# Seven of 24 key tiles exponentiated on VectorE, and reloads with earlier priorities, in a planned four-block transformer kernel

## The chip, the cores and the metric

One core of a Trainium2 chip runs the whole program in one launch. The metric is the device time of one execution in microseconds (us), taken as the median of three runs.

## The reference

Four residual blocks follow each other on x of 2048 rows by 1024 columns in bf16: linear attention (A), softmax attention (B), A and B again, with the same weights the second time. Each block first applies a layer norm. There are 32 heads of 32 columns.

```python
# block A
pq = einsum("bhsd,hdf->bhsf", q, w_phi); pk = einsum("bhsd,hdf->bhsf", k, w_phi)
phi_q = concat([softmax(pq), softmax(-pq)]); phi_k = concat([softmax(pk), softmax(-pk)])
kv = einsum("bhsf,bhsd->bhfd", phi_k, v);  z = sum over s of phi_k
o = (phi_q @ kv) / (phi_q . z + 1e-6);     x = x + o @ wo
# block B
scores = q @ k^T * 32**-0.5;  x = x + (softmax(scores) @ v) @ wo
```

For the change it matters that a key tile of block A needs two exponentials, exp(k) and exp(-k), and that block B needs the exponential of 32 x 2048 x 2048 scores each time.

## The kernel before

The program isn't written in the order in which it runs. Every operation (a group of matmuls, an activation, a DMA) is recorded with an engine, a duration that the planner assumes, the operations it depends on, its buffers and a priority; `Sched.run` then lays them out in time, and the instructions are issued in the order that this planner found. A buffer comes from one SBUF arena or from the eight PSUM banks, with a quota for each class. So a number in the table at the top of the file (a due time, a step, a limit) can shift the order of everything that follows. Each engine then runs its own list strictly in order, and waits where an operand isn't there.

Attention (block B) is cut into 32 turns, one for each pair of a 512-row query chunk and a group of four heads. A turn has 64 score tiles of 128 keys by 512 queries. TensorE makes three or four of them at once, each in 32 rows of the array (L1280). ScalarE takes the exponentials of two or three score tiles in one instruction (L1338, 128x1024 or 128x1536). One or two more tiles of a group go to VectorE, which converts them with a tensor_scalar (L1436) to 16-bit numbers whose bits are a power of two; when two such tiles have come together, `exp_dve` mends the mantissa with two masks (L1241) and two tensor_tensors (L1246). Score matrices are scaled by 2^7/ln 2 for that, and ScalarE's exponential is given the factor `e_scale` that undoes it. Then TensorE multiplies with the values and with ones (L1479). `MIX` says how many groups must lie between two groups in which ScalarE gets two tiles and VectorE the third; `MOST` limits VectorE's tiles in a turn.

TensorE's time between the scores is filled with other matmuls (L642, four at once in 32 columns each): key, value and query projections of later heads, output projections, and, in the first attention alone, the keys and values of the second linear layer. Those are made for three row chunks with eight key tiles each, 24 in all, by `a_keys` with `alone`: TensorE makes the tile, VectorE copies it out of PSUM (L874), ScalarE takes both exponentials (L878), VectorE sums them by head (L882), inverts the sums (L885) and scales the values by them (L891), and TensorE adds to the state (L913). The fourth chunk is made after the first attention, with the first layer's method. Where the planner sees TensorE with too little to do, it adds matmuls that nobody reads: four at once on `onesD` or `zero`, one at a time on `onesD` (L642, L1737, L1732, each reading `xR`).

A turn ends with VectorE's copy of the result out of PSUM (L1494) and, by a detour through DRAM (`rd`), a division: L1541 multiplies by the inverse that SyncE's queue brought back (L1528, L1534, L1536). The output projection is added to the residual in L1212. All DMAs are issued from SyncE's one queue. Ahead of the second linear layer's queries it reads back slabs of the folded query weights (`wd_q`, eight DMAs) and two chunks of normed rows (`xd`, eight DMAs, L1609).

## Time and profile before

| | before |
|---|---|
| median of three runs | 2135.45 us (2132.93 to 2135.77) |
| the profiled execution's own time | 2136.92 us |
| its span, first to last instruction | 2135.1 us |
| mean granted clock of TensorE | 0.996 |
| busy: TensorE, ScalarE, VectorE | 2086.7, 1904.7, 1772.2 us |

The stretches of the span: up to 310 us the first linear layer and what leads into attention; 310 to 1163 us the first attention; 1163 to 1390 us the rest of the second linear layer; 1390 to 2122 us the second attention; then the last output tiles. Busy times are of the hardware profiler; an activation's record reaches into that of the next one, so single durations add up to more than the busy time of the engine. The spacing of starts tells what one costs. A granted clock below 1 means that TensorE's matmuls were slowed.

### The profile page before, as it was taken

To read this page: it belongs to the slowest core of one execution; us is meant where nothing else is said; L and a number is where in the kernel's file an instruction comes from. 1 tells how busy PE (TensorE), PEld (TensorE's weight loads), DVE (VectorE), ACT (ScalarE), POOL (GpSimd) and SP (SyncE) were. 2 spreads that over 40 slices of the span, in tenths; PEclk is the share of its full clock that TensorE was granted. 3 is DMA by queue.
4 is the path that set the end of the run, shared out by engine and by line. 5 is a ranking of instruction groups with operands and counts; after the bars stand their busy time and mean duration, and the time that the engine had idled before them with its cause. 6 is when DMAs were issued, how large, how long until landed. Compare 5 with 4: busy or idle time off the path is not lost. (4 is left out here: it accounts for less than half of the span.)

```text
span 2135.1 us, 65137 instructions
## 1 busy us (share of the span) xinstructions
PE 2086.7 (98%) x27811; PEld 787.5 (37%) x27811; DVE 1772.2 (83%) x3305; ACT 1904.7 (89%) x2029; POOL 26.6 (1%) x83
## 2 busy tenths in 40 slices
PE   8999999999999999999999999999999999999999
PEld 5543443333333333333333434533333333333333
DVE  8866545757566899999998876698899999999998
ACT  7437769989999999999999577799999999999998
POOL 1000000000000000000000000000000000000000
PEclk9999999999999999999999999999999999999999
DMA  8720321131233322442455403211111122121111
GB/s 234 163 72 21 94 58 29 34 73 49 61 76 96 101 86 75 132 144 66 102 155 153 112 27 83 70 28 32 33 45 43 42 51 63 47 75 52 51 47 37
DMA packets 255467, 160.78 MB, mean 75 GB/s; under 512 B 147784, under 2 KB 229704, under 8 KB 255176
## 3 DMA queue, kind: packets, MB, share of 16 engines
q1 hardware_dynamic: 255176, 156.62, 27.5%
q8 instruction: 217, 3.56, 0.7%
q14 instruction: 74, 0.61, 0.1%
HBM read 89.72 MB, written 29.87 MB: 56 GB/s over the span
## 5 line engine op out<-in xcount | busy, mean ns | idle before, releaser
L1338 ACT ACTIVATE arena<-psum 128x1536 bf16<-128x1536 f32 (+1 forms) x1332 | 1559.3, 1437 | 28.0 <-PE psum L1280 20.0
L642 PE MATMUL psum<-arena 128*32 128x512 bf16 (+1 forms) x9536 | 634.6, 366 | 10.7 <-DVE arena L1212 2.6
L1479 PE MATMUL psum<-arena 128*32 128x512 bf16 x4096 | 606.3, 383 | 1.8 <-DVE arena L1494 1.4
L1479 PE MATMUL psum<-arena,ones_bf 128*32 128x512 bf16 x4096 | 606.4, 383 | 0.0
L1280 PE MATMUL psum<-arena 32*128 32x512 bf16 x4096 | 524.5, 384 | 24.9 <-ACT arena L1338 17.6
L1436 DVE TENSOR_SCALAR arena<-psum 128x512 uint16<-128x512 f32 x662 | 444.8, 681 | 80.9 <-PE psum L1280 76.6
L638 PE MATMUL psum<-arena 128*128 128x512 bf16 (+1 forms) x1968 | 430.5, 373 | 0.9 <-DMA arena<-in_A_wqkv_dram 0.4
L1280 PEld LDWEIGHTS <-arena 32*128 32x128 bf16 x4096 | 160.5, 91 | 551.8 <-issue 548.1
L642 PEld LDWEIGHTS <-arena 128*32 128x32 bf16 x9536 | 209.4, 95 | 262.2 <-issue 163.9
L638 PEld LDWEIGHTS <-arena 128*128 128x128 bf16 x1968 | 185.9, 98 | 220.4 <-issue 22.1
L1241 DVE TENSOR_SCALAR work<-arena 128x1024 uint16<-128x1024 uint16 (+1 forms) x668 | 261.8, 414 | 2.3
L1479 PEld LDWEIGHTS <-arena 128*32 128x32 bf16 x4096 | 167.7, 95 | 213.1 <-issue 146.9
L1246 DVE TENSOR_TENSOR arena<-work 128x1024 bf16<-128x1024 bf16 x334 | 225.7, 676 | 2.6
L1246 DVE TENSOR_TENSOR work<-arena,work 128x1024 bf16<-128x1024 bf16 x334 | 225.5, 675 | 0.0
L1479 PEld LDWEIGHTS <-ones_bf 128*32 128x32 bf16 x4096 | 166.1, 95 | 22.3 <-issue 4.0
L878 ACT ACTIVATE arena<-psum 128x512 bf16<-128x512 f32 x80 | 43.7, 595 | 75.1 <-PE psum L638 69.9
L1143 DVE CAST arena<-psum 128x512 bf16<-128x512 f32 (+1 forms) x120 | 69.2, 577 | 43.3 <-PE psum L642 43.2
L1494 DVE COPY arena<-psum 128x512 f32<-128x512 f32 x126 | 85.8, 681 | 11.5 <-PE psum L1479 11.4
L882 DVE TENSOR_REDUCE arena<-arena 128x32 f32<-128x1024 bf16 x64 | 77.4, 1209 | 16.0 <-ACT arena L878 14.3
L1038 ACT ACTIVATE arena<-psum 128x512 bf16<-128x512 f32 x112 | 60.7, 617 | 26.4 <-PE psum L638 22.5
L891 DVE TENSOR_TENSOR arena<-psum,arena 128x1024 bf16<-128x1024 f32 x64 | 78.1, 1220 | 2.6
L683 ACT ACTIVATE arena<-xR 128x1024 bf16<-128x1024 bf16 x40 | 42.4, 1065 | 36.4 <-DVE xR L1117 36.4
(103 smaller groups left out, 997.7 us busy)
## 6 DMA issues: line engine op xcount, KB each, us to landing
arena<-in_B_wqkv_dram SPq DMA_DIRECT2D x66, 256.0 KB
arena<-rd SPq DMA_DIRECT2D x62, 256.0 KB
xa<-arena SPq DMA_DIRECT2D x48, 256.0 KB
arena<-in_A_wqkv_dram SPq DMA_DIRECT2D x40, 256.0 KB
arena<-in_B_wo_dram SPq DMA_DIRECT2D x40, 256.0 KB
arena<-arena SPq DMA_DIRECT2D x256, 32.0 KB
arena<-wd_k SPq DMA_DIRECT2D x32, 256.0 KB
arena<-arena SPq DMA_DIRECT2D x62, 128.0 KB
```

The costliest lines, as they stand in the source:

```text
L638: nc.tensor.matmul(out_, lhsT=lhsT, rhs=rhs, start=start, stop=stop, skip_group_check=True)
L642: nc.tensor.matmul(out_[ks, :], lhsT=lhsT[:, ks], rhs=rhs, start=start, stop=stop, tile_position=(0, 32 * k), skip_group_check=True)
L882: red = op("DVE", dve_us(1024) + 0.107, lambda ev=ev, sv=sv: nc.vector.reduce_sum(out=sv(), in_=ev().rearrange("p s (h d) -> p (s h) d", d ...
L891: ml = op("DVE", dve_us(1024), lambda vpv=vpv, wv_=wv_, sv=sv: nc.vector.tensor_tensor(out=wv_()[:, :, :, 0:DH], in0=vpv().rearrange("p (h ...
L1143: return soon(op("DVE", dve_us(n), lambda: nc.vector.tensor_copy(out=dst(), in_=src()), [dep], bufs, prio))
L1241: return sch.later("DVE", n * C512 / 3840 + 0.065, lambda: nc.vector.tensor_scalar(out=out_().bitcast(U16), in0=y_v().bitcast(U16), scalar ...
L1246: return sch.later("DVE", n * C512 / 1920 + 0.065, lambda: nc.vector.tensor_tensor(out=out_(), in0=in0(), in1=in1(), op=what), deps, [e_b, ...
L1280: nc.tensor.matmul(out=out_, lhsT=kT[g][1]()[r, pp, d * P:(d + 1) * P], rhs=q_of[(qc, g)][1]()[r, (pp + j // 2) % 2, :], start=True, stop= ...
L1338: ex = make("ACT", act_us(w * C512), lambda: nc.scalar.activation(out=e_v()[:, 0:w * C512], in_=s_v()[:, 0:w * C512], func=ACT.Exp, scale= ...
L1436: pair["got"].append(sch.later("DVE", dve_us(512), lambda: nc.vector.tensor_scalar(out=e_v().bitcast(U16)[:, k, :], in0=s_v(), scalar1=EXP ...
L1479: nc.tensor.matmul(out=a_v()[col:col + 32, :], lhsT=v_v()[:, kc % 4, o:o + DH] if what == 0 else ones_bf[:], rhs=ev()[:, x * C512:(x + 1) ...
L1494: cp = op("DVE", dve_us(512), lambda t_v=t_v, a_v=a_v: nc.vector.tensor_copy(out=t_v(), in_=a_v()), [last], [a_b, t_b], prio - 4)
```

## The change

Seven key tiles (the last three of chunk 0, the last three of chunk 1, the last of chunk 2) don't go to ScalarE. VectorE converts the key tile straight out of PSUM, makes the negated one from it, and runs `exp_dve` on both at once. For this the folded key weights are scaled by 2^7/ln 2 in `fold_phi`, by the same 16 evictions as before, and the exponentials that stay on ScalarE use `e_scale` and its negative.

```diff
+KEY_DVE = (3, 3, 1, 0)
+XR = 40
+SL = 30
-MIX = (lambda i: (1, 2, 1, 0)[i // 8], lambda i: (0, 0, 1, 0)[i // 8])
+MIX = (lambda i: (1, 2, 1, 2)[i // 8], lambda i: (0, 0, 1, 0)[i // 8])
-MOST = (lambda i: 1 if i < 1 else 12, lambda i: 24 if i < 1 else 29)
+MOST = (lambda i: 3 if i < 1 else 12, lambda i: 24 if i < 1 else 27)
-END = 32
+END = 28
-         "e": 6, "vp": 6, "e1": 4, "vp1": 4, ...
+         "e": 6, "vp": 6, "e1": 5, "vp1": 4, ...
...
+                by_dve = alone and 4 * fc + t >= 8 - KEY_DVE[c]
+                if by_dve:
+                    k1 = op("DVE", dve_us(512), lambda kpv=kpv, ev=ev: nc.vector.tensor_scalar(
+                        out=ev().bitcast(U16)[:, 0, :], in0=kpv(), scalar1=EXP2_OFF * ONE, scalar2=0.0,
+                        op0=ALU.add, op1=ALU.max), [k1], [kp, eb], pr)
+                    soon(k1)
+                elif alone:
...
-                ex = [op("ACT", act_us(512), lambda s=s, kpv=kpv, ev=ev: nc.scalar.activation(
-                    out=ev()[:, s, :], in_=kpv(), func=ACT.Exp, scale=(1.0, -1.0)[s]),
+                ex = [] if by_dve else [op("ACT", act_us(512), lambda s=s, kpv=kpv, ev=ev: nc.scalar.activation(
+                    out=ev()[:, s, :], in_=kpv(), func=ACT.Exp, scale=(e_scale, -e_scale)[s]),
...
+                        n = sch.later("DVE", C512 / 3840 + 0.065, lambda: nc.vector.tensor_scalar(
+                            out=ev().bitcast(U16)[:, 1, :], in0=ev().bitcast(U16)[:, 0, :], scalar1=-1.0,
+                            scalar2=2 * EXP2_OFF * ONE, op0=ALU.mult, op1=ALU.add), [o], [eb], pr)
+                        exp_dve({"got": [o, n], "bufs": (eb,), "e": ev}, pr).out.append(red)
...
-            wq_s = [slab("slab", second - 15 + fc, ...
+            wq_s = [slab("slab", second - SL + fc, ...
-                xnA[c] = (x_b, x_v, [dma(second - 20 + 20 * c, ...
+                xnA[c] = (x_b, x_v, [dma(second - XR + 20 * c, ...
```

Some fifteen more numbers of the table change by a little: due times of the second attention's key, value and late query tiles (KS, VH, V_LATE, Q_LATE), of output projections (GAPS, OUT_AT, GO, WO), and limits (SLACK, OPEN, MOST_E, NEAR).

What the planner makes of it, counted in the two built programs:

| | before | after |
|---|---|---|
| ScalarE, three score tiles in one (L1338, 128x1536) | 770 | 812 |
| ScalarE, two score tiles in one (128x1024) | 562 | 518 |
| ScalarE, exponentials of keys (L878) | 128 | 114 |
| VectorE, score tiles converted (L1436) | 662 | 624 |
| VectorE, pairs mended (two L1241, two L1246 of 128x1024) | 328 | 315, seven of them keys |
| VectorE, single tiles mended | 6 | 8 |
| TensorE, passes of three or four scores | 1332 | 1330 |
| TensorE, unread passes: onesD in columns, zero, onesD whole | 111, 51, 47 | 90, 64, 45 |

All of the difference in ScalarE's and nearly all in VectorE's counts lies in the first attention; the second has 368 and 283 of ScalarE's two kinds in both programs. Of the first attention's 32 turns the last sixteen have 41 more of the three-tile kind, 42 fewer of the two-tile kind and 41 fewer score tiles on VectorE. All other matmuls are the same in number, in another order from the first turns on. On SyncE's queue the eight `wd_q` reads now stand ahead of the last-but-one turn's `rd` write (L1534), where all eight stood behind it; the eight `xd` reads stand where they stood, behind the last `qf` and `in_B_wqkv` reads.

VectorE, chunk 1's sixth key tile, in turn 24, lines of before: the key tile is copied (L874), and summed (L882) when ScalarE has made its exponentials; the products of an earlier tile (L891) lie between.

```order
L874 COPY arena<-psum 128x512
L1436 TENSOR_SCALAR arena<-psum 128x512
L1246 TENSOR_TENSOR work<-arena,work 128x1024
L1436 TENSOR_SCALAR arena<-psum 128x512
L882 TENSOR_REDUCE arena<-arena 128x32
L891 TENSOR_TENSOR arena<-psum,arena 128x32x32
L885 RECIPROCAL arena<-arena 128x32
```

The same tile of VectorE after the change, where L1260 and L1265 are the masks and products of `exp_dve`, L1455 a score tile, and L891, L910 and L904 the sum, the scaled values and the inverse:

```order
L878 TENSOR_SCALAR arena<-psum 128x512
L899 TENSOR_SCALAR arena<-arena 128x512
L1260 TENSOR_SCALAR work<-arena 128x1024 x2
L1265 TENSOR_TENSOR work<-arena,work 128x1024
L1265 TENSOR_TENSOR arena<-work 128x1024
L1455 TENSOR_SCALAR arena<-psum 128x512
L891 TENSOR_REDUCE arena<-arena 128x32
L910 TENSOR_TENSOR arena<-psum,arena 128x32x32
L904 RECIPROCAL arena<-arena 128x32
```

A conversion stands in the copy's place, and five instructions more stand between it and the sum.

ScalarE in the last quarter of the first attention, before, from 1090 us of the span on; the width tells whether two or three score tiles are taken:

```order
L1338 ACTIVATE arena<-psum 128x1536
L1338 ACTIVATE arena<-psum 128x1024 x4
L1338 ACTIVATE arena<-psum 128x1536 x2
L878 ACTIVATE arena<-arena 128x512 x2
L1338 ACTIVATE arena<-psum 128x1536 x2
L1338 ACTIVATE arena<-psum 128x1024 x2
L1338 ACTIVATE arena<-psum 128x1536
L1338 ACTIVATE arena<-psum 128x1024 x5
```

ScalarE at about the same place after the change (L1357 is L1338, L887 is L878):

```order
L1357 ACTIVATE arena<-psum 128x1536
L1357 ACTIVATE arena<-psum 128x1024
L1357 ACTIVATE arena<-psum 128x1536 x2
L1357 ACTIVATE arena<-psum 128x1024
L1357 ACTIVATE arena<-psum 128x1536 x2
L887 ACTIVATE arena<-arena 128x512 x2
L1357 ACTIVATE arena<-psum 128x1024
```

With MIX at 2 one two-tile instruction is followed by two of three tiles; before they could follow each other.

VectorE where the first attention ends, before: L1541 is the division of the turn before the last, which needs the `rd` read; L1212 evicts an output projection; L1494 is the last turn's copy, and L1504 its inverse.

```order
L1212 TENSOR_TENSOR arena<-xR,psum 128x512
L1246 TENSOR_TENSOR arena<-work 128x1024
L1541 TENSOR_TENSOR arena<-arena 128x512
L1212 TENSOR_TENSOR arena<-xR,psum 128x512
L1494 COPY arena<-psum 128x512
L1504 RECIPROCAL arena<-arena 64x128 x2
```

VectorE at the same place after the change (L1231 is L1212, L1513 is L1494, L1523 is L1504, L1560 is L1541):

```order
L944 TENSOR_TENSOR arena<-arena,psum 128x264
L1552 RECIPROCAL arena<-arena 128x16
L1231 TENSOR_TENSOR arena<-xR,psum 128x512 x2
L1513 COPY arena<-psum 128x512
L1523 RECIPROCAL arena<-arena 64x128 x2
L1231 TENSOR_TENSOR arena<-xR,psum 128x512
L1560 TENSOR_TENSOR arena<-arena 128x512
```

The division that needs the read now stands behind three evictions, the last copy and two inversions.

More of the change, by code (lines that the diff above doesn't have):

```diff
@@ L438 @@
 KL = (17.0, 31.56)
-KS = (2.41, 4.25)
+KS = (2.41, 5.55)
 VS = (4.26, 6.75)
@@ L447 @@
 LN_PE = (3, 3)
[L448 removed]
+WO = 8.18
 KD = 12.15
 HALF = (False, True)
[L451 to L453 removed]
+VH = 3.31
+V_LATE = (None, ((21.96, 6.48), (59.37, 7.17)))
+Q_LATE = (lambda c, g: 104.52 + 4.56 * g if c == 2 else -5.67 + 18.61 * g, lambda c, g: 151.84 + 11.78 * g)
 QL = (11, 9.91)
 AW = 26
[L456 to L457 removed]
+OUT_AT = (228.3, 247.14, 267.11)
+GO = 3.17
 BO = 296.78
@@ L752, in turned_slab, with fold_phi @@
         return b, v, [got[0] + got[1], got[2] + got[3]] * 2
-    def fold_phi(col, wd_v, prio, use_pe, after=()):
+    def fold_phi(col, wd_v, prio, use_pe, after=(), by=1.0):
         w_t = []
@@ L800, in fold_phi @@
                 if eng == "ACT":
-                    e = op("ACT", act_us(512), lambda m=m, pv=pv, s_v=s_v: nc.scalar.copy(
-                        out=s_v()[:, m, :], in_=pv()), [a], [pb, s_b], prio + 0.01)
-                else:
-                    e = soon(op("DVE", dve_us(512), lambda m=m, pv=pv, s_v=s_v: nc.vector.tensor_copy(
-                        out=s_v()[:, m, :], in_=pv()), [a], [pb, s_b], prio + 0.01))
+                    e = op("ACT", act_us(512), lambda m=m, pv=pv, s_v=s_v: nc.scalar.activation(
+                        out=s_v()[:, m, :], in_=pv(), func=ACT.Copy, scale=by), [a], [pb, s_b], prio + 0.01)
+                else:
+                    e = soon(op("DVE", dve_us(512), lambda m=m, pv=pv, s_v=s_v: nc.vector.tensor_scalar(
+                        out=s_v()[:, m, :], in0=pv(), scalar1=by, scalar2=None, op0=ALU.mult), [a], [pb, s_b], prio + 0.01))
                 parts.append(e)
@@ L1604 @@
         else:
-            wq_s = [slab("slab", second - 15 + fc, wdq_v[:, :, fc * C512:(fc + 1) * C512], C512, [store["q"][fc]])
+            wq_s = [slab("slab", second - SL + fc, wdq_v[:, :, fc * C512:(fc + 1) * C512], C512, [store["q"][fc]])
                     for fc in range(2)]
```

32 lines of the change are left out of this document (15 added, 17 removed).

## The prediction, as it was put on record

> **What bounds the kernel now.** I read the view of windows first, one window for each stage; the two middle columns that matter are busy us of VectorE (third) and ScalarE (fourth), the one before the last but one is TensorE's granted clock. The chain of waits is of no use here: it follows the last eleven microseconds alone.
>
> ```profile
> core 0: us, PE busy (x) PEld busy (x) DVE busy (x) ACT busy (x) POOL busy (x), PEclk, DMA share, GB/s
> 310.00:540.00 230.00, 227.17 (x3111) 78.92 (x3109) 144.34 (x262) 215.74 (x184) 0.00 (x0) 1.00 0.19 47
> 540.00:744.00 204.00, 199.44 (x2779) 65.45 (x2776) 136.76 (x254) 201.50 (x168) 0.00 (x0) 0.99 0.31 84
> 744.00:855.00 111.00, 105.67 (x1590) 36.95 (x1594) 103.12 (x184) 107.09 (x103) 3.16 (x8) 1.00 0.28 79
> 855.00:960.00 105.00, 101.64 (x1491) 33.50 (x1483) 97.74 (x181) 101.06 (x96) 1.83 (x4) 0.98 0.49 140
> 960.00:1066.00 106.00, 104.04 (x1682) 37.02 (x1680) 105.77 (x201) 102.48 (x98) 1.58 (x4) 1.00 0.32 83
> 1066.00:1163.00 97.00, 93.66 (x1539) 33.28 (x1539) 93.67 (x169) 94.89 (x93) 3.06 (x8) 1.00 0.50 135
> 1163.00:1390.00 227.00, 222.67 (x2055) 97.91 (x2058) 162.17 (x301) 156.31 (x291) 2.81 (x8) 0.98 0.31 84
> 1390.00:2122.00 732.00, 717.34 (x10555) 253.84 (x10547) 703.84 (x1366) 731.66 (x631) 0.00 (x0) 1.00 0.17 46
> ```
>
> Three regimes. In the second attention (1390 to 2122) ScalarE is busy for 731.66 of 732 us: it is the bound, and there is nothing else to win. From 540 to 744 VectorE has a third of its time free, and ScalarE, at 201.50 of 204, still sets the pace. From 744 to 1163, where key tiles of the second linear layer are made, all engines are near full: VectorE 103.12 + 97.74 + 105.77 + 93.67 = 400.3 of 419 us, in one window 105.77 of 106; ScalarE 107.09 + 101.06 + 102.48 + 94.89 = 405.5. ScalarE's idle 13.5 us there are what a better balance could win.
>
> What ended that idle time, in the view of waits for ScalarE from 744 to 1163 us (us in total, times, longest):
>
> ```profile
> ACT arena L1338 <- PE psum L1280: 9.0, 13, 2.1
> ACT arena L1338 <- PE psum L642: 1.7, 3, 1.1
> ACT arena L1338 <- PE psum L1479: 1.6, 2, 1.2
> ```
>
> ScalarE waits for scores, so for TensorE. TensorE's records overlap, so its share of busy time says little; the timeline of TensorE gives the price of a pass by starts:
>
> ```profile
> 1501.63 0.39 PE L1280 MATMUL psum<-arena 32*128 32x512 bf16 x3
> 1501.95 1.05 PE L642 MATMUL psum<-arena 128*32 128x512 bf16 x16
> 1502.93 0.39 PE L1280 MATMUL psum<-arena 32*128 32x512 bf16 x3
> ```
>
> Sixteen column matmuls are four passes. Scores to the next kind take 0.32 us, four passes and the change back 0.98: with two equal changes of kind that is about 0.22 a pass and 0.10 a change.
>
> **The change part by part.** First the balance of 744 to 1163. The timelines of ScalarE and VectorE price one instruction (start, time, count):
>
> ```profile
> 977.08 4.13 ACT L1338 ACTIVATE arena<-psum 128x1536 bf16<-128x1536 f32 x3
> 984.78 2.90 ACT L1338 ACTIVATE arena<-psum 128x1024 bf16<-128x1024 f32 x3
> 1089.81 1.34 ACT L878 ACTIVATE arena<-arena 128x512 bf16<-128x512 f32 x2
> 1090.85 8.00 ACT L1338 ACTIVATE arena<-psum 128x1536 bf16<-128x1536 f32 x7
> ...
> 982.51 0.41 DVE L1241 TENSOR_SCALAR work<-arena 128x1024 uint16<-128x1024 uint16 x1
> 982.85 0.68 DVE L874 COPY arena<-psum 128x512 f32<-128x512 f32 x1
> 983.45 0.67 DVE L1436 TENSOR_SCALAR arena<-psum 128x512 uint16<-128x512 f32 x1
> 984.05 0.67 DVE L1246 TENSOR_TENSOR work<-arena,work 128x1024 bf16<-128x1024 bf16 x1
> 984.65 0.68 DVE L1436 TENSOR_SCALAR arena<-psum 128x512 uint16<-128x512 f32 x1
> ...
> L1241 DVE TENSOR_SCALAR work<-arena 128x512 uint16<-128x512 uint16 x12 | 3.0, 282 | 0.0
> ```
>
> ScalarE: three tiles in one cost 4.13 / 3 = 1.38 us, two tiles 2.90 / 3 = 0.97, a key's exponential (1090.85 - 1089.81) / 2 = 0.52. In the whole program 42 more of the first, 44 fewer of the second, 14 fewer of the third: 58.0 - 42.7 - 7.3 = **8.0 us more** work, nearly all in the last sixteen turns, so in 744 to 1163.
>
> VectorE: a conversion costs 0.60 by starts, as a copy does, so the seven conversions in place of seven copies are free. A key tile adds the negation (0.28 at most, the length of the 512-wide mask), two masks of 0.34 and two products of 0.60: 2.16, times seven 15.1 us. Off go 38 score conversions, 22.8, and 20 pairs (the 13 by which the count falls and the seven that are now keys) of 1.88, 37.6; two more single tiles add about 2. Sum: **43 us less**, of 400.3.
>
> So VectorE is no longer near its limit there (some 357 of 419), and ScalarE is: 405.5 + 8.0 = 413.5 us of work. The end of this stretch is then set by how much ScalarE idles. The nearest regime is 540 to 744, with VectorE at two thirds and ScalarE at 201.50 of 204: idle 1.2%, which gives 413.5 x 1.012 = 418.5, a gain of 0.5. The second attention idles 0.34 of 732, which gives 413.7, a gain of 5.3. With all of the idle 13.5 kept it is 427, a loss of 8.0. I take about the middle of the first two, **a gain of 2.5**: the window from 540 to 744 holds a stop of TensorE for a late weight slab, and without it would be nearer the second attention's value.
>
> ```profile
> 607.67 0.40 PE L642 MATMUL psum<-arena 128*32 128x512 bf16 x4 [1.54 <-DMA arena<-in_B_wqkv_dram]
> ```
>
> Both ends, -5.3 and +8.0, are kept for the range.
>
> TensorE's own share moves little: 23 passes that nobody reads go, 13 come, and 1332 score passes become 1330: 10 + 2 passes of 0.22, 2.6 us, which either filled gaps or lie within the term above. It isn't counted again.
>
> A rule that speaks against part of the change: the Trainium skill, Perfetto Trace Analysis, section Optimizing Scalar/DVE Operations, says that work which either engine can do may go to ScalarE when VectorE is saturated. The seven key tiles go the other way, into windows with VectorE at 105.77 of 106; by the rule alone they would cost their 15.1 us there. The windows show ScalarE just as full, and the score tiles that leave outweigh them, so the sum doesn't use the rule.
>
> Second, the end of the first attention, where the changed order matters:
>
> ```profile
> 1162.54 0.69 DVE L1541 TENSOR_TENSOR arena<-arena 128x512 bf16<-128x512 f32 x1 [2.80 <-DMA arena<-rd]
> 1163.33 0.69 DVE L1212 TENSOR_TENSOR arena<-xR,psum 128x512 f32<-128x512 bf16 x1
> 1164.07 0.83 PE L642 MATMUL psum<-arena 128*32 128x512 bf16 x12 [2.04 <-DVE arena L1212]
> ...
> 1137.91 11.37 SPq L1528 DMA_DIRECT2D arena<-arena  x4
> 1140.00:1150.00 10.00, 10.00 (x157) 3.44 (x145) 10.00 (x17) 9.10 (x11) 0.32 (x1) 1.00 0.01 3
> 1160.00:1170.00 10.00, 7.96 (x98) 2.37 (x95) 6.84 (x9) 7.14 (x6) 0.00 (x0) 0.83 0.96 292
> ```
>
> VectorE stood 2.80 us at a division whose operand was still on its way from DRAM, in a stretch with the DMA engines at 0.96. Behind it in VectorE's list stood an eviction (L1212), for whose PSUM bank TensorE waited 2.04 us. Then the clock fell: 0.83 over 10 us is 3.4 us at half speed, 1.7 us lost. In the new order that division stands behind three evictions, the last copy and two inversions, and the eight slab reads stand ahead of the `rd` write. They fit there: SyncE's queue spent 11.37 us on four small copies that waited for VectorE, and the DMA engines were busy for 0.01 of 1140 to 1150. So what TensorE waited for no longer waits for DRAM. What is late next is the division itself, which nobody but the output projection of that chunk needs. I count 2.04 + 1.7 = **3.7 us gained**; the least is 0 (another wait takes its place), the most these 3.7.
>
> The Trainium skill, TensorE: Matmul & The Clock Gate, section HAM oscillation — how this bites in real kernels, says that the clock falls after TensorE has idled for more than about 3.4 us. By that rule this wait would have cost 2.0 and not 3.7; the trace shows the half clock behind a wait of 2.04 us, and the trace decides.
>
> Third, what costs nothing: the scale in the key weights rides in the 16 evictions that were there; `e_scale` is an operand of the same activation. A key tile's sum comes later by five VectorE instructions, some 2.2 us; the conversion waits for TensorE as the copy did, and the sum for VectorE's own work only, so nothing is held up behind it in VectorE's list; waiting for it are the inverse and the scaled values, which the state matmuls of a chunk half need only after four tiles, and one more buffer (e1 5) holds the tile meanwhile. If that cover were gone, it is 7 x 2.2 = 15 us at most. The earlier priority of the `xd` reads has no effect: they stand where they stood in the queue. The second attention has the same ScalarE instructions in number and kind and is bound by ScalarE, so it stays within its 0.34 us of idle, or gets worse where the shifted due times open a new wait.
>
> **The sum**: 2.5 + 3.7 = 6.2 us less. The profiled execution had 2136.92 us, a span of 2135.1 and 1.8 around it; 2136.92 - 6.2 = 2130.7. It lies 1.5 above the median of the three runs, so on that scale I predict 2135.45 - 6.2 = **2129.3 us**.
>
> **The rivals.** (a) ScalarE becomes the bound without losing its idle time: TensorE's filler matmuls between scores still come late, as the 9.0 us of waits for L1280 show, and VectorE's relief doesn't change that. Then 8.0 is added from 744 to 1163, and with the 3.7 gained the time is 2139.8; if the end of the attention doesn't gain either, 2143.5. It decides as soon as more than 9.2 of ScalarE's 13.5 us of idle time remain (8.0 + 9.2 - 13.5 = 3.7). For it: the waits name TensorE, not VectorE. Against it: with VectorE at two thirds, 540 to 744 idles 1.2%.
>
> (b) The order is new from 320 us on, and a new order has its own stops: a wait of some 2 us with the clock behind it costs 3.7, wherever it falls. Two windows with 0.98 and one with 0.99 above hold such stops now. If the new order has the same number, with one in place of that at 1163, only the balance remains: 2135.45 - 2.5 = 2133.0, which is no measurable difference.
>
> (c) More is won: the balance gains 5.3, the end 3.7, and one more stop of 3.7 goes: 2122.8.
>
> (d) The change doesn't do what it says: for the `xd` reads that is so already. If the `wd_q` reads, 2 MB put ahead, delay the `rd` write more than they did, the 3.7 become 0, as in (b).
>
> **How the numbers follow.** A measurement of this kernel tells about 0.2% from no change, 4.3 us, so faster means below 2131.2 and slower above 2139.7. My forecast (2125 to 2131.2) has 0.39, (c) with all below 2125 0.12, (b) and (d), between 2131.2 and 2139.7, 0.27, (a), above, 0.22. Faster 0.51, same 0.27, slower 0.22. The range takes in (c) and (a) with the 3.7 gained and stops short of (a) without: 2121 to 2142.
>
> **What would show it.** In the windows of the changed kernel VectorE should be busy for about 85% of the stretch in which the first attention's last sixteen turns run, ScalarE for 98% or more, and the stretch should be 2 to 3 us shorter; rival (a) shows as ScalarE's idle above 9 us there. VectorE's division may wait for `rd` at the end of the first attention, but no eviction and no matmul behind it, and the clock should not fall there. The second attention should last 732 us within 1. I am wrong on the mechanism if the time is won or lost after 1390 us, or before 744.

## The result, and the profile after

The changed kernel takes 2136.98 us (median of 20 runs, 2131.32 to 2142.21), the one before 2132.64 us beside it (20 runs, 2129.94 to 2137.22): ratio 1.0019, with a 95% interval of 1.0013 to 1.0025. That is some 4 us slower (3 to 5 by the interval): a small change, but the wrong way round, for the forecast was 2129.3 us, 6.2 us faster.

The profile on which the prediction was worked out had a span of 2135.1 us, above what before takes in most runs; a second profile of the unchanged kernel, with a span of 2129.2 us, is the better partner (label r_before, see the experiments). Here is its view of windows, with the columns of the prediction's first fence. The cuts follow the program and not the clock: first exponential of the first attention, VectorE's copies that end its 16th and its 24th turn, last exponential, first and last exponential of the second attention.

```profile
310.90:745.90 435.00, 426.65 (x5884) 143.93 (x5883) 281.46 (x514) 418.06 (x352) 0.00 (x0) 1.00 0.25 64
745.90:957.30 211.40, 205.20 (x3074) 70.69 (x3073) 200.49 (x362) 206.33 (x198) 4.95 (x12) 1.00 0.38 111
957.30:1165.70 208.40, 203.38 (x3302) 72.16 (x3301) 206.06 (x377) 202.42 (x193) 4.65 (x12) 1.00 0.41 113
1165.70:1363.00 197.30, 192.30 (x1662) 89.12 (x1680) 135.23 (x253) 130.45 (x268) 2.81 (x8) 1.00 0.31 86
1363.00:2116.70 753.70, 738.03 (x10860) 261.56 (x10857) 724.91 (x1405) 753.06 (x651) 0.00 (x0) 1.00 0.17 45
```

The same five windows of the changed kernel (its profiled execution took 2134.18 us, with a span of 2132.4, so 2.8 us less than its median):

```profile
309.90:741.10 431.20, 425.10 (x5894) 144.76 (x5892) 279.71 (x509) 417.05 (x351) 0.00 (x0) 1.00 0.25 64
741.10:960.70 219.60, 210.64 (x3097) 71.20 (x3093) 197.49 (x360) 212.19 (x195) 4.18 (x11) 0.98 0.37 109
960.70:1166.50 205.80, 198.35 (x3231) 70.29 (x3232) 172.29 (x303) 204.51 (x180) 4.86 (x13) 1.00 0.40 115
1166.50:1366.40 199.90, 192.82 (x1682) 89.78 (x1702) 137.08 (x255) 131.50 (x267) 2.58 (x8) 1.00 0.31 83
1366.40:2119.80 753.40, 735.74 (x10841) 260.56 (x10845) 725.65 (x1409) 752.85 (x651) 0.00 (x0) 1.00 0.17 45
```

Compare the second number of each row, the length of the stretch. The first sixteen turns are 3.8 us shorter, turns 17 to 24 are 8.2 longer, the last eight 2.6 shorter, the stage between the attentions 2.6 longer, the second attention the same. So the last sixteen turns, where the key tiles moved, lose 5.6 us (425.4 for 419.8), and the place is in the first half of them, where the clock column falls to 0.98.

The first profile of the kernel before, cut at the same events, has for turns 17 to 24 and 25 to 32:

```profile
744.60:959.80 215.20, 206.99 (x3077) 70.34 (x3074) 200.06 (x363) 207.35 (x197) 4.98 (x12) 0.99 0.38 109
959.80:1171.00 211.20, 204.82 (x3297) 72.35 (x3299) 206.04 (x377) 202.70 (x194) 4.65 (x12) 0.99 0.42 115
```

Its last exponential starts at 1171 us, so the first attention ends there and not at 1163. Its last sixteen turns take 426.4 us, 6.6 more than those of r_before, with the same instructions in the same order. So two executions of the kernel before differ there by about as much as the forecast gain of 6.2.

The changed kernel's engines are as the forecast had them. ScalarE is busy 212.19 + 204.51 = 416.7 us against 408.75 (8.0 more), VectorE 369.8 against 406.6 and so 87% of the stretch. What did not come is the fall of ScalarE's idle time (the stretch less ScalarE's busy time): 8.7 us are left of 11.1. The view of ScalarE's waits from 744 to 1163 us in the changed kernel (us in total, times, longest) says for whom:

```profile
ACT arena L1357 <- PE psum L1299: 4.1, 5, 1.3
ACT arena L1357 <- DMA xa<-arena: 1.7, 1, 1.7
ACT arena L1357 <- PE psum L645: 1.2, 1, 1.2
```

Waits for TensorE's scores, 4.1 us where the prediction's view had 9.0, and a new one: for a DMA. The timeline shows two stops of TensorE in turns 17 to 24 (in brackets the idle time ahead, and behind the arrow what ended it):

```profile
833.20 0.34 SPq L1553 DMA_DIRECT2D rd<-arena  x1
...
834.22 1.86 SPq L1547 DMA_DIRECT2D arena<-arena  x2
...
836.18 0.53 SPq L743 DMA_DIRECT2D arena<-in_B_wo_dram  x1
...
836.82 0.58 SPq L1555 DMA_DIRECT2D arena<-rd  x1
...
837.49 0.93 SPq L743 DMA_DIRECT2D arena<-in_B_wo_dram  x2
...
843.99 0.61 PE L645 MATMUL psum<-arena 128*32 128x512 bf16 x8 [1.50 <-DMA arena<-in_B_wo_dram]
...
886.44 1.55 SPq L726 DMA_DIRECT2D xa<-arena  x3
...
894.19 3.28 ACT L1357 ACTIVATE arena<-psum 128x1024 bf16<-128x1024 f32 x3 [1.67 <-DMA xa<-arena]
...
895.27 0.40 PE L1299 MATMUL psum<-arena 32*128 32x512 bf16 x3 [1.92 <-ACT arena L1357]
```

At 844 TensorE waits for a part of the output projection's weight slab. Three of the slab's four reads stood in SyncE's queue behind the write of a turn's reciprocals (L1553), for which the queue waited 3.9 us for VectorE, and behind copies (L1547). At 894 ScalarE may not write its exponentials, because their place in SBUF still holds a row tile whose write to DRAM, issued before 888, has not ended; TensorE waits for ScalarE in turn. Behind both the clock falls, which the windows of 10 us around them show (column PEclk: 0.83 is 3.4 us at half speed):

```profile
840.00:850.00 10.00, 8.48 (x98) 2.15 (x90) 8.20 (x16) 8.38 (x8) 0.00 (x0) 0.83 0.30 92
890.00:900.00 10.00, 8.08 (x98) 2.22 (x90) 7.92 (x15) 8.07 (x8) 0.00 (x0) 0.85 0.35 107
```

### The profile page after: what moved, and what is told of

Same layout as the page of the kernel before. It is cut to its first block, busy times and chain, and to the rows that moved or that the text cites. A ratio compares the mean times of both kernels' runs of the same rounds, so it can differ in the third digit from the quotient of the medians.

```text
span 2132.4 us, 64940 instructions
## 1 busy us (share of the span) xinstructions
PE 2073.9 (97%) x27711; PEld 787.8 (37%) x27777; DVE 1737.1 (81%) x3230; ACT 1911.6 (90%) x2013; POOL 25.7 (1%) x83
## 4 chain that ended last, share of the span: by engine, by line
PE 50%; ACT 27%; DVE 13%; issue 6%; DMA 3%; SPq 0%; ACTq 0%; DVEq 0%
ACT arena L1357 25%; PE psum L641 17%; PE psum L645 12%; PE psum L1498 9%; PE psum L1299 9%; DVE arena L1455 4%; DVE work L1260 2%; DVE work L1265 2%; DVE arena L1265 1%; DMA arena<-rd 1%; DVE arena L1513 1%; PE psum L932 1%; DMA arena<-arena 1%; ACT arena L887 1%; DMA arena<-in_A_wqkv_dram 1%
## 5 line engine op out<-in xcount | busy, mean ns | idle before, releaser
L1357 ACT ACTIVATE arena<-psum 128x1536 bf16<-128x1536 f32 (+1 forms) x1330 | 1573.7, 1473 | 18.6 <-PE psum L1299 13.0
L1455 DVE TENSOR_SCALAR arena<-psum 128x512 uint16<-128x512 f32 x624 | 423.4, 685 | 112.0 <-PE psum L1299 96.1
L641 PE MATMUL psum<-arena 128*128 128x512 bf16 (+1 forms) x1907 | 421.6, 372 | 10.0 <-issue 5.6
L1260 DVE TENSOR_SCALAR work<-arena 128x1024 uint16<-128x1024 uint16 (+1 forms) x646 | 253.2, 415 | 2.6
L1265 DVE TENSOR_TENSOR arena<-work 128x1024 bf16<-128x1024 bf16 x323 | 218.3, 676 | 2.8
L1265 DVE TENSOR_TENSOR work<-arena,work 128x1024 bf16<-128x1024 bf16 x323 | 218.3, 676 | 0.0
L887 ACT ACTIVATE arena<-psum 128x512 bf16<-128x512 f32 x80 | 43.7, 595 | 76.0 <-PE psum L641 69.9
L891 DVE TENSOR_REDUCE arena<-arena 128x32 f32<-128x1024 bf16 x64 | 77.5, 1211 | 20.9 <-ACT arena L887 19.1
L1513 DVE COPY arena<-psum 128x512 f32<-128x512 f32 x126 | 85.9, 682 | 9.3 <-PE psum L1498 9.0
L910 DVE TENSOR_TENSOR arena<-psum,arena 128x1024 bf16<-128x1024 f32 x64 | 78.2, 1221 | 4.4 <-PE psum L1498 1.6
```

The source lines that it names most:

```text
L641: nc.tensor.matmul(out_, lhsT=lhsT, rhs=rhs, start=start, stop=stop, skip_group_check=True)
L891: red = op("DVE", dve_us(1024) + 0.107, lambda ev=ev, sv=sv: nc.vector.reduce_sum(out=sv(), in_=ev().rearrange("p s (h d) -> p (s h) d", d ...
L910: ml = op("DVE", dve_us(1024), lambda vpv=vpv, wv_=wv_, sv=sv: nc.vector.tensor_tensor(out=wv_()[:, :, :, 0:DH], in0=vpv().rearrange("p (h ...
L1260: return sch.later("DVE", n * C512 / 3840 + 0.065, lambda: nc.vector.tensor_scalar(out=out_().bitcast(U16), in0=y_v().bitcast(U16), scalar ...
L1265: return sch.later("DVE", n * C512 / 1920 + 0.065, lambda: nc.vector.tensor_tensor(out=out_(), in0=in0(), in1=in1(), op=what), deps, [e_b, ...
L1357: ex = make("ACT", act_us(w * C512), lambda: nc.scalar.activation(out=e_v()[:, 0:w * C512], in_=s_v()[:, 0:w * C512], func=ACT.Exp, scale= ...
```

## The experiments

Two theories stood against each other. **Theory S**: the changed order brings stops of its own, and these are the loss. **Theory A**: ScalarE, with 8 us more to do, is the bound, and the loss is its work; a stop taken away would only show up as idle time elsewhere. Each kernel was timed beside the kernel before, and a ratio is always to that.

**r_before**: the kernel before, unchanged.

> The kernel before once more, unchanged, for a second profile and the clocks of its runs. Theory S (stops): the executions of one kernel differ by the number of times that TensorE stops for a late DMA and its clock then falls; each such stop costs about 3.7 us, so time falls as the mean clock rises, about 2 us for each 0.001, and at equal clock the kernel before and the changed one are within 1 us. Theory A (ScalarE): the changed kernel has 8 us more ScalarE work in 744 to 1163 us and is longer there at any clock, by 4 us or more. This profile should show a median-like span of about 2131 us with fewer of the half-clock windows than the first profile of before had (four after the start).

2132.00 us against 2132.13, ratio 0.9998 (0.9989 to 1.0007). So this much two sets of runs of one kernel differ. The profile's span is 2129.2 us, and between 310 us and the end it has one stretch of half clock (at 610 us), where the first profile had four. It also shows the place on which a term of the prediction rested, the division that waits for `rd` at the end of the first attention:

```profile
1158.90 0.69 DVE L1541 TENSOR_TENSOR arena<-arena 128x512 bf16<-128x512 f32 x1 [1.10 <-DMA arena<-rd]
...
1159.69 0.69 DVE L1212 TENSOR_TENSOR arena<-xR,psum 128x512 f32<-128x512 bf16 x1
...
1160.44 0.83 PE L642 MATMUL psum<-arena 128*32 128x512 bf16 x12 [0.34 <-DVE arena L1212]
```

The instructions stand as they did, but the wait is 1.10 us here, where it was 2.80, and TensorE loses 0.34 where it lost 2.04. When the reciprocals land differs between executions. The stop was real, but not in every run.

**r_after**: the changed kernel, unchanged.

> The changed kernel once more, unchanged. Theory S: a span of about 2135 us in the typical run with three to five half-clock windows after the start, where the first profile had two at 2132.4; at equal mean clock no slower than before. Theory A: slower at equal clock, by 4 us, and longer in the last sixteen turns of the first attention.

2136.27 us, ratio 1.0019 (1.0009 to 1.0028). Its profiled execution is again one of the faster ones, with a span of 2131.8 us. Its last sixteen turns take 425.5 us, as in the first profile, with the same two stops and a third, at 1088:

```profile
1076.29 0.58 SPq L1555 DMA_DIRECT2D arena<-rd  x1
...
1083.64 0.69 DVE L1560 TENSOR_TENSOR arena<-arena 128x512 bf16<-128x512 f32 x1 [1.61 <-DMA arena<-rd]
...
1086.58 1.22 DVE L910 TENSOR_TENSOR arena<-psum,arena 128x1024 bf16<-128x1024 f32 x1
...
1087.85 0.83 PE L645 MATMUL psum<-arena 128*32 128x512 bf16 x12 [1.57 <-DVE arena L910]
```

Behind the stop near 844 there is no half clock in this execution, behind that near 893 there is, and the window of 10 us around the third has 3.4 us of it:

```profile
1085.00:1095.00 10.00, 7.90 (x93) 2.25 (x89) 8.39 (x14) 7.89 (x8) 0.33 (x1) 0.83 0.39 117
```

It is the mechanism that the prediction counted as gone, at another place: a division waits for `rd`, an instruction that frees a PSUM bank stands behind it in VectorE's list, and TensorE waits for the bank. In the first profile it was there too, with 0.98 us of TensorE and no fall of the clock.

Neither theory has the times at equal clock right. At a mean clock of 0.998 the changed kernel's runs average 2134.3 us (nine runs of its two sets) and those of the kernel before 2132.6 (59 runs of all its sets): some 2 us apart, where theory S allows 1 and theory A asks for 4. So a part of the loss goes with the clock, and a part is there without it.

**e_nokey**: the changed kernel with all key tiles on ScalarE.

```diff
-KEY_DVE = (3, 3, 1, 0)
+KEY_DVE = (0, 0, 0, 0)
```

> The changed kernel with no key tile on VectorE (KEY_DVE all 0), all other numbers as changed. Theory A: the 14 exponentials come back to ScalarE, 7.3 us more there less what the planner hands to VectorE in exchange, so about 2 to 7 us slower than the changed kernel. Theory S: only the order is shuffled; within 3 us of the changed kernel either way, with the difference in the half-clock windows.

2148.79 us, ratio 1.0072 (1.0056 to 1.0088), about 12 us slower than the changed kernel. Turns 25 to 32 and the stage behind the attention, in its windows:

```profile
952.60:1165.80 213.20, 205.59 (x3363) 74.27 (x3363) 175.04 (x298) 210.82 (x195) 5.55 (x16) 1.00 0.41 120
1165.80:1379.50 213.70, 205.02 (x1787) 94.19 (x1805) 139.53 (x258) 132.01 (x268) 2.59 (x8) 0.98 0.31 85
```

ScalarE is at 210.82 of 213.20 us, and the stage after the attention has grown from 199.9 to 213.7: TensorE work that found no place beside the attention is done behind it (1787 matmuls there for 1682). Neither theory's figure holds, 2 to 7 us or within 3. With the new tables, VectorE's share of the key tiles is needed.

**e_noahead**: the changed kernel with the reloads' due times as before.

```diff
-XR = 40
-SL = 30
+XR = 20
+SL = 15
```

> The changed kernel with the old priorities of the reloads (20 and 15 in place of 40 and 30). If the wait for rd at the end of the first attention is what the earlier wd_q reads spare, the stop of 2 us and the half clock near 1163 us come back: 3.7 us slower than the changed kernel. If the order of VectorE's list alone spares it: the same time as the changed kernel within 1.5 us.

2141.19 us, ratio 1.0040 (1.0026 to 1.0054). The program is the changed one's up to 1138 us, where that issues its `wd_q` reads. Behind that, the stage between the attentions takes 203.0 us for 199.9, and the second half of the second attention 384.1 for 381.6. In the stage between, the timeline shows a wait that the changed kernel has in neither profile, ScalarE's for a read of `qf`, and TensorE's for ScalarE:

```profile
1190.56 0.63 ACT L1057 ACTIVATE arena<-arena 128x512 bf16<-128x512 f32 x1 [4.56 <-DMA arena<-qf]
...
1192.14 1.47 PE L641 MATMUL psum<-arena 128*128 128x512 bf16 x6 [2.27 <-ACT arena L722]
```

The stop near 1163 us, with which the expectation reckoned, did not come back. The eight `xd` reads stand at the same place in both queues; the `wd_q` reads do not. Seven of the eight now stand behind the `rd` write, six of them ahead of the last four `qf` reads, and these are issued from 1185.1 us on instead of 1175.6 (some 3 us of this are stops before 1138 us). So the earlier `wd_q` reads, with the order that follows from them, are worth some 4 us, by another wait than the one counted; no wait is known for the 2.5 us in the second attention.

**x_div**: the changed kernel, its planned order kept but for one instruction. The planner's list is edited before it is issued: the division seen at 1083.64 goes behind the next three of VectorE, which puts it just ahead of L910.

```diff
-    for o in sch.run():
+    done = sch.run()
+    by = {o.seq: o for o in done}
+    def behind(a, b):
+        done.remove(by[a])
+        done.insert(done.index(by[b]) + 1, by[a])
+    behind(3770, 4839)
+    for o in done:
         o.fn()
```

> The changed kernel with one instruction in another place: the VectorE division L1560 that waits at 1083 to 1084 us for its reciprocals (rd) stands behind the next three VectorE instructions (L1265, L1455, L891) and so just ahead of L910, whose bank TensorE waits for at 1088. All else in the order of the changed kernel. Theory S (the 4 us of the changed kernel over the one before are mostly TensorE stops that its plan brings, each with what ScalarE then idles): the stop of 1.4 to 2.0 us at 1088 and, where it comes, the half clock behind it go, and with them the 0.7 to 2.8 us that ScalarE idles at 1086 to 1092; 2134.5, ratio about 1.0011. Theory A (ScalarE has 9.2 us more to do in the last sixteen turns and is the bound there; a removed stop only moves its idle time to the next place): within 0.5 us of the changed kernel, 2136.2, ratio 1.0019.

2134.74 us, ratio 1.0009 (1.0000 to 1.0018): 2 us less than the changed kernel's 1.0019, near theory S's figure, but its interval meets that of the changed kernel. In its profile the stop at 1088 is down to 1.03 us from one matmul's start to the next. But one of 1.97 us, with half clock behind it, stands at 757 us, where VectorE's inversion L1552 waits 1.88 us for copies of its operand, and the last sixteen turns are no shorter than in r_after, 426.6 for 425.5. The stop at 757 is in all three profiles with this edit (x_div, x_three, x_four) and not in x_two or the two of the changed kernel as it is; why is open.

**x_two**: the stops at 844 and 894 taken away in the same manner: three reads of the w_o slab behind the first, and two row tiles change places in SBUF.

```diff
+    for a, b in ((4067, 4066), (4068, 4067), (4069, 4068)):
+        behind(a, b)
+    p, q = by[4527].bufs[0], by[4533].bufs[0]
+    p.at, q.at = q.at, p.at
```

> The changed kernel without the stops at 843 and 893 us: the last three of the four reads of the w_o slab of that place (L743) stand right behind the first in SP's list, ahead of the reciprocals' writes and reads that they stood behind; and the first and the last of the four normalized row tiles written at 882 to 886 us change places in SBUF, so that the exponential that waited at 890 us for the last tile's write gets the place of the first one. Theory S: the stops of 1.7 to 1.9 and 2.2 to 2.3 us go with the half clock behind them and ScalarE's idle time of 1.3 to 2.7 us there and 2.8 to 3.0 us here; 2136.3 - 4.8 = 2131.5, ratio about 0.9997. Theory A: the idle time comes back elsewhere, less than 1 us is gained, 2135.5 or more, ratio 1.0015 or more.

2131.18 us, ratio 0.9994 (0.9985 to 1.0003): 5 us less, outside the changed kernel's interval. Theory A, with 1.0015 or more, falls. Both stops are gone from the profile, and its last sixteen turns take 421.1 us.

**x_three**: both edits together.

> The changed kernel with both edits of the two other runs, so without the stops at 843, 893 and 1088 us. Theory S: 2136.3 - 4.8 - 1.8 = 2129.7, ratio about 0.9989, faster than the kernel before. Theory A: 2135 or more, ratio 1.0013 or more. If the gains of the two other runs do not add up here, the idle time of one place moves to another.

2130.70 us, ratio 0.9992 (0.9983 to 1.0001). The timeline of its profile at the three places:

```profile
829.57 4.28 SPq L743 DMA_DIRECT2D arena<-in_B_wo_dram  x4
...
882.45 12.94 ACT L1357 ACTIVATE arena<-psum 128x1536 bf16<-128x1536 f32 x11
...
1082.66 0.68 DVE L1560 TENSOR_TENSOR arena<-arena 128x512 bf16<-128x512 f32 x1
...
1083.26 1.22 DVE L910 TENSOR_TENSOR arena<-psum,arena 128x1024 bf16<-128x1024 f32 x1
...
1084.53 0.83 PE L645 MATMUL psum<-arena 128*32 128x512 bf16 x12 [0.65 <-DVE arena L910]
```

And the windows of 10 us around them:

```profile
840.00:850.00 10.00, 9.77 (x135) 3.23 (x131) 10.00 (x20) 10.00 (x10) 0.00 (x0) 1.00 0.16 50
888.00:898.00 10.00, 9.63 (x131) 3.12 (x131) 9.89 (x19) 9.99 (x10) 0.00 (x0) 1.00 0.45 141
1080.00:1090.00 10.00, 8.83 (x133) 2.92 (x121) 9.25 (x16) 10.00 (x11) 0.34 (x1) 1.00 0.49 161
```

The reads of the slab are all issued by 833.9 us, where the last ended at 838.4, some 5 us earlier; ScalarE runs eleven exponentials on end over the place where it waited; the division no longer waits, and TensorE waits 0.65 us. ScalarE is busy all of the three windows, the clock is whole. Four instructions in another place and two buffers exchanged, with no work taken away, give 2136.27 - 2130.70 = 5.6 us, all of the loss and a little more. The last sixteen turns take 420.7 us in this profile, 4.7 fewer than in the changed kernel's first. The two gains (2.1 and 5.3 us by the ratios) add up to more than that, within their intervals.

**x_b608**: the same treatment for the kernel before, whose stop at 607 us the prediction had quoted: one weight slab is read some 5 us earlier.

```diff
+    behind(2187, 2995)
```

> The kernel before with one read of a weight slab (L739, seen at 601.9 to 603.2 us) issued some 5 us earlier, ahead of four L1135 copies and the read of the reciprocals in SP's list, so that TensorE's stop of 1.9 to 2.1 us at 607 to 609 us goes, with the half clock behind it. Theory S: ScalarE's idle time of 2.8 to 3.0 us at 605 to 615 us is won: 2132.1 - 2.9 = 2129.2, ratio 0.9986; then the 4 us that the changed kernel wins in its first sixteen turns are in the main this stop, and could be had without the change. Theory A: the first sixteen turns are bound by ScalarE's work and the idle time comes back before their end; less than 1 us, ratio 0.9996 or more.

2130.11 us, ratio 0.9987 (0.9979 to 0.9996). The slab's read in the timeline of x_b608, and its window:

```profile
597.96 0.53 SPq L739 DMA_DIRECT2D arena<-in_B_wqkv_dram  x1
```

```profile
605.00:615.00 10.00, 9.81 (x144) 3.51 (x140) 5.83 (x11) 10.00 (x9) 0.00 (x0) 1.00 0.41 93
```

The same window of r_before:

```profile
605.00:615.00 10.00, 8.23 (x98) 2.19 (x94) 2.62 (x4) 7.55 (x7) 0.00 (x0) 0.83 0.52 128
```

ScalarE gains 2.45 of 10 us, and the kernel 2.5. The changed kernel has no stop there: of the 3.8 us that it wins in the first sixteen turns, most is this (x_b608 has 431.6 us there, r_before 435.0).

**x_four**: x_three, and the four reads of normalized rows that TensorE waited for at 876 us ahead of three copies.

```diff
+    for a, b in ((5009, 4497), (5010, 5009), (5011, 5010), (5012, 5011)):
+        behind(a, b)
```

> The changed kernel without the stops at 843, 893 and 1088 us, as in the run before it, and with one edit more: the four reads of normalized rows (L1741, issued at 868.8 to 870.4 us) stand ahead of the three copies to q2 (L1198 to L1200) that hold them up in SP's list, so that they are issued some 2.5 us earlier and TensorE's wait of 1.0 to 1.7 us at 876 us for them goes. Theory S: ScalarE's idle time of about 1.2 us there is won, 2130.7 - 1.2 = 2129.5, ratio 0.9986. Theory A: nothing is left to win in this stage, since ScalarE idles only 5.6 us of 215 there; 2130.7, ratio 0.9992.

2129.32 us, ratio 0.9984 (0.9976 to 0.9993): faster than both kernels. By itself the fourth edit is within the uncertainty. The last sixteen turns:

```profile
740.50:954.70 214.20, 207.94 (x3097) 71.34 (x3093) 196.63 (x360) 211.49 (x195) 4.19 (x11) 1.00 0.38 111
954.70:1160.30 205.60, 198.49 (x3231) 70.44 (x3232) 172.45 (x303) 204.39 (x180) 4.84 (x13) 1.00 0.40 115
```

ScalarE is busy 415.9 of 419.8 us: 3.9 us idle, 0.9%.

**x_b2**: x_b608, and three reads of a slab that nobody needs yet behind those of the w_o slab, to let the reciprocals of 1158 us land earlier.

```diff
+    for a, b in ((5300, 4221), (5301, 5300), (5302, 5301)):
+        behind(a, b)
```

> The kernel before without its stop at 608 us, as in the run x_b608, and with one edit more: three reads of 256 KB for the second layer's slab (L740, issued at 1149.9 to 1151.7 us around the read of the reciprocals L1536) are issued some 10 us later, behind the reads of the w_o slab, so that the reciprocals land earlier and VectorE's division L1541 no longer waits 2.5 us at 1156 to 1158 with an eviction behind it that TensorE waits for. Theory S: that stop of 2.1 us, in two of three profiles of before, goes with the 1.7 to 3.3 us that ScalarE idles at it: 2130.1 - 1.7 = 2128.4, ratio 0.9980; so the kernel before, rid of two stops, is faster than the changed one rid of three or four, and the change in itself is worth nothing or a little less. Theory B (the change in itself, its stops apart, is worth 2 us or more): x_b2 is not faster than x_four.

2129.34 us, ratio 0.9980 (0.9971 to 0.9989). In its profile TensorE waits 0.49 us at that place, where it waited 1.73 in the profile of x_b608. The last sixteen turns take 419.7 us:

```profile
743.70:954.60 210.90, 205.50 (x3074) 70.76 (x3073) 200.22 (x362) 206.36 (x198) 4.97 (x12) 1.00 0.39 112
954.60:1163.40 208.80, 203.35 (x3304) 72.12 (x3299) 206.16 (x377) 202.60 (x193) 4.66 (x12) 1.00 0.40 109
```

Rid of the stops that were edited, both kernels stand level, 2129.32 and 2129.34 us, and their last sixteen turns too, 419.8 and 419.7: one with ScalarE busy 415.9 us and 3.9 idle, the other with 409.0 and 10.7. By theory S x_b2 would have been faster, by theory B x_four; the intervals allow a difference of some 2 us either way and no more. The level is a sum: in these profiles x_four is 2.4 us shorter in the first sixteen turns, where x_b2 has a stop at 480 us, and 2.6 longer between the attentions, where x_four has one at 1199 that no edit touched.

**e_mixold**: the changed kernel, with the last eight turns' exponentials dealt out as before.

```diff
-MIX = (lambda i: (1, 2, 1, 2)[i // 8], lambda i: (0, 0, 1, 0)[i // 8])
+MIX = (lambda i: (1, 2, 1, 0)[i // 8], lambda i: (0, 0, 1, 0)[i // 8])
```

> The changed kernel with the table MIX of the kernel before, which gives the exponentials of the last eight turns of the first attention back to VectorE: VectorE gets some 42 us of exponentials more in the last sixteen turns and ScalarE some 14 us less; the key tiles stay with VectorE. Theory T (the engines' totals decide): VectorE has about what it had in the kernel before there and ScalarE 5 us less, 2130 to 2135, ratio 0.999 to 1.001. Theory F (what decides is how many of the second layer's projections and key tiles fit beside the attention, and each key tile needs four VectorE instructions, so some slip behind it): the attention ends no later, the stage between the attentions is 15 to 20 us longer, 2150 to 2156, ratio 1.008 to 1.011.

2158.95 us, ratio 1.0118 (1.0104 to 1.0132). Theory T falls; theory F has the direction and the place, and its 2150 to 2156 is too low, as are its 15 to 20 us for the stage. The last eight turns are no longer, and the stage behind them is 224.1 us:

```profile
961.50:1163.30 201.80, 194.72 (x3033) 67.25 (x3036) 199.31 (x372) 194.49 (x183) 5.58 (x12) 1.00 0.37 106
1163.30:1387.40 224.10, 214.57 (x1999) 97.76 (x1994) 148.51 (x270) 131.11 (x268) 3.09 (x9) 0.98 0.31 85
```

TensorE ran some 200 matmuls fewer in the eight turns and some 300 more behind them. VectorE is at 199.31 of 201.80.

**e_keyonly**: the kernel before with the seven key tiles on VectorE, and all tables and due times as before.

```diff
-        ... lambda ...: nc.scalar.copy(out=..., in_=pv())
+        ... lambda ...: nc.scalar.activation(out=..., in_=pv(), func=ACT.Copy, scale=by)
...
+KEY_DVE = (3, 3, 1, 0)
-         "e": 6, "vp": 6, "e1": 4, ...
+         "e": 6, "vp": 6, "e1": 5, ...
```

> The kernel before with one part of the change alone: seven key tiles get both exponentials from VectorE (with the scale of the folded weights that this needs, and five of e1's buffers), all tables and due times as before. Theory T (totals): ScalarE 7 us less and VectorE 16 us more work in the last sixteen turns, where VectorE was busy 95% of the time, so 3 to 8 us longer, 2135 to 2140, ratio 1.001 to 1.004. Theory F (fills): attention 1 ends some 10 us earlier and the stage between the attentions is 25 to 31 us longer, 2149 to 2153, ratio 1.008 to 1.010.

2158.31 us, ratio 1.0117 (1.0102 to 1.0133): the same picture, with 229.1 us between the attentions; theory F's 2149 to 2153 is too low again. Either half alone is 17 (e_nokey) to 25 us slower than the kernel before; together, stops apart, they come out even. In these tables, then, the halves need each other. That no other table would carry one half alone is not shown: every due time is set for the whole, each of these edits makes the planner lay out everything anew, and no table was fitted to a half.

## Why the prediction failed, step by step

**What was right.** VectorE's 43 us less are 36.8, and its 85% is 87%. The second attention is the same, 753.4 for 753.7 us. At the end of the first attention itself the forecast order did what was said: in both profiles of the changed kernel the division (L1560, at 1164.6) no longer waits, and TensorE has no stop of more than 1 us from 1151 to 1202 us.

**Right in part by luck.** ScalarE's 8.0 us more are 8.0 by busy time. But the prices of 1.38 and 0.97 us are a row's duration divided by its count, and that takes in the tail of the last record. The median spacing of starts is 1.33 and 0.90 us, and with the counts of the last sixteen turns (41 more, 42 fewer, 14 key exponentials fewer) the work is 9 us more. Busy time too counts the tail ahead of each gap, so it shows less idle time than there is.

**The balance, "a gain of 2.5": the step that failed by most.** The forecast let the stretch go from 419 to 416.5 us, with 413.5 of work, and so let ScalarE's idle time fall from 13.5 us to 3.0. The stretch became 5.6 us longer, 8.1 off. Of these, 2.4 lie in the start: 13.5 was one execution's idle time, and r_before has 11.1 in the sixteen turns. The other 5.7 are idle time that stayed, 8.7 for 3.0. The reason is not ScalarE's rate: with the three stops mended (x_three) the idle time is 4.5 us and the stretch 420.7, and x_four has 3.9, 0.9%, about the 1.2% read from 540 to 744 us. Even so nothing is won: 419.8 us in x_four and in r_before, 7.1 of work more and 7.1 of idle time less. So the step that failed is to take the idle share of another stretch and charge the new order no stops of its own. The prediction had them as rival (b), but with as many as before and one in place of that at 1163; there were three in these turns. Rival (a) just misses its own mark (above 9 us of idle time; the two profiles have 8.7 and 9.0), and theory A, which is its stronger form, fell in x_two.

**The end of the first attention, "3.7 us gained".** The wait went, but the gain was not there to be had in most runs: in r_before TensorE loses 0.34 us at that place, with no half clock behind it. The forecast took one execution's stop as a gain in every run. The same chain of division and bank then stopped TensorE at 1088. The price of 3.7 for a stop was high as well: 5.6 us for three.

**What costs nothing.** "The earlier priority of the `xd` reads has no effect" is borne out by e_noahead's queue. The earlier `wd_q` reads do gain some 4 us, near the 3.7 forecast for the end of the attention, but elsewhere, in part at ScalarE's wait for `qf`: that nearness is luck.

**What was not in the sum.** 3.8 us won in the first sixteen turns, mostly the stop at 607 that the prediction quoted for another purpose. They are won before 744 us, which the prediction named as a sign of a wrong mechanism. And 2.6 us lost between the attentions, where TensorE stops for about 2 us near 1205 us in both profiles of the changed kernel and in neither of the kernel before; that this stop is the loss was not tried.

The accounts, by windows: -3.8 first sixteen turns, +5.6 last sixteen, +2.6 between, -0.3 second attention, with the lead-in 1.0 shorter: +3.1, and the spans differ by 3.2. The medians differ by 4.3. The rest may lie in stops that come in some runs only, as both profiled executions of the changed kernel are among its faster ones: the mean granted clock is 0.9969 and 0.9975 in its two sets of runs, 0.9980 in r_before and 0.9985 in x_four, and 0.001 of the span is 2 us. That is argued and not shown.

## What to carry to other kernels

When a change gives a near-full kernel a new order, forecast the balance of the engines and the stops apart: the balance can be worked out from counts and prices, while the stops of the new order can't be seen in the trace of the old one, and here they decided the sign. Before a stop's end is counted as a gain, look whether a second execution has it: here two executions of one kernel differed by 6.6 us in the very turns in which 6.2 were to be won; before a change is judged, look whether its loss is a handful of waits, since a late read or a reused buffer can be mended by moving one instruction.

## What the runs showed of the hardware

Short stops can bring the half clock, but not all do. In fourteen profiles, between 310 and 1400 us, TensorE had 39 stops of 1.8 to 3.1 us from one matmul's start to the next; 22 were followed by a stretch of half clock. Such a stretch lasts 3.41 us, or in four cases, all between the attentions, 6.83. Two stops of the changed kernel's first profile (the idle time in brackets is a little shorter than the distance of the starts, 2.31 and 2.61 us):

```profile
895.27 0.40 PE L1299 MATMUL psum<-arena 32*128 32x512 bf16 x3 [1.92 <-ACT arena L1357]
...
1205.12 2.12 PE L641 MATMUL psum<-arena 128*128 128x512 bf16 x9 [2.42 <-issue]
```

The window around the second, the longer one, has a whole clock, where that around the first (above) has 0.85:

```profile
1200.00:1210.00 10.00, 7.52 (x158) 3.96 (x158) 5.41 (x8) 2.05 (x4) 0.58 (x2) 1.00 0.01 3
```

The Trainium skill, TensorE: Matmul & The Clock Gate, section The HAM clock gate (the "warmup" mystery), says that a free-running window of 4096 cycles watches TensorE. That the same stop falls under the gate in one run and not in another agrees with it: the one near 845 us, 1.89 us long, has half clock behind it in the changed kernel's first profile, and one of 1.99 us at that place in x_div has none. That a stop of 1.69 us is enough in one profile (x_b608, at 866 us) does not agree with the Trainium skill's rule for idle gaps of 3.4 us that the prediction cites.

A division began 7.4 us after the read of its operand was issued (1076.29 to 1083.64 in r_after, with writes of rows on the way). At the end of the kernel before's first attention the wait for such a read was 2.80 us in one execution and 1.10 in another.
